# Fused attention and two feed-forward layers: a split first part for two experts instead of one, and an earlier second half of one chunk's routing

## The chip, the core and the metric

The kernel runs on one core of a Trainium2 chip. A core has five engines with instruction queues of their own: TensorE (PE) for matmuls, VectorE (DVE), ScalarE (ACT), GpSimd (POOL) and SyncE (SP), which here only issues DMAs. The metric is the device time of one execution in microseconds (us); lower is better.

## The reference

Attention whose mask keeps a query and a key together only when they fall into the same hash bucket, then a dense feed-forward layer (512 to 2048 to 512), then eight experts of which each token uses two. The last part is where the change lies:

```python
logits = x @ w_gate
noisy_logits = logits + np.log1p(np.exp(x @ w_noise)) * noise
top2 = np.argpartition(-noisy_logits, 2, axis=1)[:, :2]
...
for e in range(E):                       # E = 8, D = 512, F = 1024
    for k in range(2):
        mask = top2[:, k] == e
        h = np.maximum(x[mask] @ w1[e], 0.0)
        out[mask] += top2_w[mask, k, None] * (h @ w2[e])
```

There are 1536 tokens. Which tokens an expert gets is known only once the routing of all tokens is done.

## The kernel before, in words

The tokens go through attention and the dense layer in six chunks of 256, numbered 0 to 5. The program is written out as numbered steps: a table `todo` says which pieces stand in which step (`at`, `soon`, `start`), and from step 100 on each engine runs its instructions in exactly the order in which the steps write them. Nothing overtakes: a wait holds whatever stands behind it on that engine.

**Dense layer.** Sixteen steps per chunk: eight of the first product (`h`, line L455), then eight of the second (`px`, L466, 12 matmuls each). After four `px` steps one half chunk of 128 tokens is ready, and ACT (L480) and DVE (L489) write it to `xr`. SP transposes it to `xrt` (`r_t`, L560), which the routing reads.

**Routing** (`route(ci)`). PE multiplies `xrt` by the gate weights (`pz`, L568 and L570), ACT copies that to `zc` (L573), and a chain of some forty small DVE and ACT instructions (`z` L576, exponentials L585 and L595, `top`, `ix`, the mask `mk` L623, the running count `cum` L625) finds the two experts of each token. PE then counts the earlier tokens of each expert (`pp`, L640 and L641), ACT copies it (`pq`, L643), DVE works out the slots (L645 to `si`, L669), and POOL scatters the rows of `xr` into a table `slots` in DRAM by four indirect DMAs (L675). The second half, from `pp` on, stands in a later step than the first.

**Experts.** Each has 400 slots. `e_load` lets SP fetch an expert's rows transposed as `xg` (L746) and their weights and token numbers as `mt` (L751, L756). `e_meta` (L766 to L776) turns `mt` into scales and indices on DVE. The items of work are listed in `seq`, one after another: for each expert eight `l1` items (`ph`, L789, 12 matmuls each), whose outputs ACT and DVE write to `ht` (L799, L800), and then one `l2` item per 128 slots (`py`, L811, L815), whose output ACT scales (L825) and POOL adds to the result (L828). Three `ph` buffers hold the outputs of `l1` items until DVE has read them.

Expert 0 is cut in two: slots 0 to 255, which `reserve` (L685 to L693) guarantees to be filled by chunks 0 to 4 alone, and slots 256 to 399. So its first part needs no routing of chunk 5. `EA` is the number of experts cut this way. The routing of chunk 5 runs between the first `l1` items, eight small pieces per item from item 2 on.

**Expert weights.** For each expert SP loads eight blocks of 512 KB into four `w32` buffers (`w12_load`, L718 and L721), and `w12_split` turns each into two half-precision parts: ACT the high one (L732), DVE the low one (L733), both named `ew`. `S1` gives the items at which the blocks of expert 1 are split; they are loaded five items earlier.

Of the kernel before, what the change touches and what calls it, by code (L numbers as in the profile page):

```python
# [17 lines left out]
B, H, S, D = 2, 8, 768, 64  # L18
# [15 lines left out]
NCH = NT // CT  # L34
# [17 lines left out]
SW2 = 2.0 ** 6  # L52


PARAM = dict(GM=16, HE=lambda nm, b: 'D', OE=lambda nm, b: 'D', SC=lambda nm, b: 'D', WB=0, XO=lambda b: 'D', NG=16, WS=lambda i: 'P', TS=lambda g: True, XL=lambda g: 'D', GW=2, E0=7, T0=12, T1=16, EL=8, WX=3, PV={(1,2,3):4}, PVD=5, ST={}, VA={}, RA={}, O0=48, OS=2, IS=2, FU=16, VF=2, EC=lambda g: 'AA', QX=8, QS=3, EA=1, S1=(8,8,8,9,9,9,11,13), QE=8, XG=2, XB=2, PC=2, OH=3, BK=3, R0=18, R1=0, LK=8, WL=1, NW=3, LE=lambda nc: nc.scalar, I0=24, LQ=8, LV=0, W=[(g, 1) for g in range(-6, 30)], KA={(0,0,0):-8,(0,0,1):-6,(0,1,0):-4,(0,1,1):-2}, QA={(0,0,0):-7,(0,0,1):-3}, HI=lambda g: 'P', LO=lambda g: False)
PARAM.update(KA={(0, 0, 0): -15, (0, 0, 1): -6, (0, 1, 0): -5, (0, 1, 1): -4, (0, 2, 0): -1, (0, 2, 1): 1, (0, 3, 0): 4, (0, 3, 1): 5, (1, 0, 0): 37, (1, 0, 1): 39, (1, 1, 0): 44, (1, 1, 1): 46, (1, 2, 0): 42, (1, 2, 1): 51, (1, 3, 0): 47, (1, 3, 1): 51}, QA={(0, 0, 0): -15, (0, 0, 1): -3, (0, 0, 2): 1, (0, 0, 3): 3, (0, 1, 0): 8, (0, 1, 1): 9, (0, 1, 2): 17, (0, 1, 3): 21, (0, 2, 0): 24, (0, 2, 1): 28, (0, 2, 2): 30, (0, 2, 3): 33, (1, 0, 0): 37, (1, 0, 1): 41, (1, 0, 2): 47, (1, 0, 3): 52, (1, 1, 0): 57, (1, 1, 1): 56, (1, 1, 2): 60, (1, 1, 3): 69, (1, 2, 0): 72, (1, 2, 1): 69, (1, 2, 2): 80, (1, 2, 3): 84}, VA={(0, 0, 0): -1, (0, 0, 1): -3, (0, 1, 0): -1, (0, 1, 1): -1, (0, 2, 0): 0, (0, 2, 1): 0, (0, 3, 0): -1, (0, 3, 1): -2, (1, 0, 0): -1, (1, 0, 1): -1, (1, 1, 0): 2, (1, 1, 1): -4, (1, 2, 0): -3, (1, 2, 1): -3, (1, 3, 0): 2, (1, 3, 1): -2}, PV={(0, 0, 0): 4, (0, 0, 1): 5, (0, 0, 2): 6, (0, 0, 3): 5, (0, 1, 0): 6, (0, 1, 1): 4, (0, 1, 2): 4, (0, 1, 3): 5, (0, 2, 0): 5, (0, 2, 1): 5, (0, 2, 2): 5, (0, 2, 3): 6, (1, 0, 0): 4, (1, 0, 1): 5, (1, 0, 2): 4, (1, 0, 3): 5, (1, 1, 0): 5, (1, 1, 1): 5, (1, 1, 2): 5, (1, 1, 3): 6, (1, 2, 0): 6, (1, 2, 1): 4, (1, 2, 2): 4, (1, 2, 3): 4}, RA={0: 18, 1: 18, 2: 19, 3: 24, 4: 18}, W=[(g,1) for g in [-6, -4, -3, -1, 0, 0, 1, 1, 2, 4, 4, 7, 8, 8, 9, 10, 11, 12, 13, 14, 15, 16, 16, 17, 18, 20, 20, 22, 22, 23, 23, 24]], EC=lambda g:'AA', LE=lambda nc:nc.sync, HI=lambda g:'AAAA'[g%4], LO=lambda g:[0, 0, 0, 1, 0, 0, 0, 1][g%8]==1, S1=[8, 8, 8, 8, 8, 11, 13, 22], ST={0: 4, 1: 4, 2: 5, 3: 4, 4: 5, 5: 3}, NG=28, WS=lambda i:'PAAA'[i%4], HE=lambda nm,b:'DPDD'[2*(nm=='k')+b], OE=lambda nm,b:'DTDD'[2*(nm=='k')+b], SC=lambda nm,b:'DADD'[2*(nm=='k')+b], R1=2, I0=16, IS=2, O0=56, OS=1, GM=100, BK=3, OH=3, QX=8, QS=2, QE=7, VF=0, T0=12, T1=17, EL=10, WX=5, WL=2, PC=2, GW=2, E0=8, WB=2)


@with_exitstack
def fused(ctx: ExitStack, tc: tile.TileContext, q, k, v, proj, w_in, w_out, w_gate, w_noise, noise,  # L60
          w1, w2, out, dbg=None):
    nc = tc.nc
# [64 lines left out]
    def stack_hi(nm, b, u):
# [17 lines left out]
        if m == "A":
# [64 lines left out]
    FU = PARAM["FU"]  # L210
# [44 lines left out]
    NG = max(PARAM["NG"], FU)  # L255
# [285 lines left out]
    EA = PARAM['EA']  # L541
# [324 lines left out]
    LK, LQ, LV = PARAM["LK"], PARAM["LQ"], PARAM["LV"]  # L866
# [43 lines left out]
    ST = [PARAM["ST"].get(ci, 3 if ci in (0, B * NCH - 1) else PARAM["PVD"] - 1) for ci in range(B * NCH)]  # L910
# [39 lines left out]
    for g in range(g_lo, G1 + 1):  # L950
# [7 lines left out]
        prev = steps.get(g - 1, [])  # L958
# [28 lines left out]
    seq, begin = [], {}  # L987
# [47 lines left out]
    with tc.If(most > CAP):  # L1035
        with tc.tile_pool(name="ov", bufs=1) as ov:
# [10 lines left out]
            x = ov.tile([128, 1024], F32)  # L1047
# [94 lines left out]
```

## Time and profile before

| | us |
|---|---|
| median of 3 runs (829.01 to 832.91) | 829.92 |
| the profiled execution | 827.38 |
| its span, first to last instruction | 825.6 |
| PE busy in the span | 716.3 (87%) |
| DVE busy | 540.1 (65%) |
| ACT busy | 442.2 (54%) |
| POOL busy | 274.8 (33%) |

The profiled execution took 1.8 us more than its span, and lies 2.5 us below the median. Times in rows count from the start of the span. The expert part begins after the last `px` matmul, at about 525 us.

### The profile page before, as it was taken

The numbers are of one execution on the slowest core, as the hardware profiler recorded it, in microseconds if no ns is written. First come the engines' busy times: TensorE is split into PE (matmuls) and PEld (weight loads), VectorE is DVE, ScalarE is ACT, GpSimd is POOL, SyncE is SP. The second block draws the span as 40 slices with busy tenths as digits, with TensorE's granted clock in tenths as the row PEclk, the third lists the DMA queues.
The fourth block names the chain that finished last, engine by engine and source line by source line (L and its number), as shares of the span: only waits on it lengthen the run. The fifth ranks groups of instructions, "written<-read, shape, count | busy, mean of one in ns | idle before, by whom it ended". The sixth has DMA issues, their size and how long they took to land. (4 is left out here: it accounts for less than half of the span.)

```text
span 825.6 us, 14780 instructions
## 1 busy us (share of the span) xinstructions
PE 716.3 (87%) x5398; PEld 445.2 (54%) x5399; DVE 540.1 (65%) x1327; ACT 442.2 (54%) x859; POOL 274.8 (33%) x304
## 2 busy tenths in 40 slices
PE   1466578787988989899999999779999999999995
PEld 1343346544764567476568576447554655555553
DVE  8998479999898889678858625454634526344210
ACT  3677666766776687567557425243533534434220
POOL 6455426653444144314402232241031120311212
PEclk9978689999999999999999999999999999999998
DMA  8999997877988996776685442857966858667213
GB/s 205 238 216 337 325 284 183 204 171 145 185 157 176 214 181 121 179 134 111 132 159 120 96 166 79 229 133 188 254 140 187 187 119 233 142 187 175 28 18 47
DMA packets 268125, 140.03 MB, mean 170 GB/s; under 512 B 224720, under 2 KB 243856, under 8 KB 268048
## 3 DMA queue, kind: packets, MB, share of 16 engines
q1 hardware_dynamic: 261520, 125.37, 63.4%
q0 software_dynamic: 6528, 13.68, 9.3%
q8 instruction: 43, 0.70, 0.4%
q14 instruction: 34, 0.28, 0.1%
HBM read 61.48 MB, written 23.79 MB: 103 GB/s over the span
## 5 line engine op out<-in xcount | busy, mean ns | idle before, releaser
L455 PE MATMUL h<-xt,wi 128*128 128x256 f16 x1152 | 142.3, 279 | 6.7 <-DVE th L485 5.0
L789 PE MATMUL ph<-xg,ew 128*128 128x400 f16 (+2 forms) x864 | 135.4, 320 | 9.3 <-DMA xg<-slots 8.8
L466 PE MATMUL px<-wo,gt 128*128 128x512 f16 x576 | 133.7, 385 | 7.2 <-ACT wo L440 4.2
L733 DVE SCALAR_TENSOR_TENSOR ew<-w,ew 128x1024 f16<-128x1024 f32 x64 | 77.9, 1226 | 89.4 <-ACT ew L732 89.2
L455 PEld LDWEIGHTS <-wi 128*128 128x128 f16 x1152 | 113.0, 100 | 29.2 <-issue 6.5
L811 PE MATMUL py<-ew,ht 128*128 128x512 f16 x576 | 125.8, 379 | 0.0
L828 POOL DMA_INDIRECT out_dram<-yo,ti x32 | 51.2, 1600 | 216.5 <-ACT yo L825 216.5
L251 PE MATMUL s<-kt,qt 128*128 128x512 f16 (+1 forms) x384 | 84.9, 343 | 35.2 <-ACT e L270 26.3
L789 PEld LDWEIGHTS <-ew 128*128 128x128 f16 x864 | 82.8, 100 | 60.2 <-issue 6.7
L270 ACT ACTIVATE e<-s,mx 128x768 f32<-128x768 f32 x96 | 86.0, 897 | 45.8 <-DVE mx L261 38.6
L500 POOL TENSOR_TENSOR gt<-th,gt 128x512 f16<-128x512 f32 x48 | 62.2, 1296 | 113.9 <-ACT gt L499 112.7
L466 PEld LDWEIGHTS <-gt 128*128 128x128 f16 x576 | 55.4, 99 | 72.5 <-issue 10.1
L811 PEld LDWEIGHTS <-ht 128*128 128x128 f16 x576 | 56.3, 98 | 67.0
L260 DVE TENSOR_REDUCE mx<-s 128x1 f32<-128x768 f32 x96 | 90.5, 948 | 2.3 <-PE s L251 2.2
L318 DVE SCALAR_TENSOR_TENSOR er<-e,mx,er 128x768 f16<-128x768 f32 x68 | 72.4, 1069 | 15.2 <-ACT er L309 15.0
L825 ACT ACTIVATE yo<-py,wv 128x512 f32<-128x512 f32 (+1 forms) x32 | 20.3, 634 | 101.9 <-PE py L811 54.5
L309 ACT ACTIVATE er<-e,mx 128x768 f16<-128x768 f32 x68 | 62.9, 933 | 20.1 <-DMA et<-er 9.5
L799 ACT ACTIVATE ht<-ph 128x400 f16<-128x400 f32 (+2 forms) x72 | 33.6, 467 | 73.7 <-PE ph L789 73.7
L251 PEld LDWEIGHTS <-qt 128*128 128x128 f16 x384 | 36.2, 101 | 64.0 <-issue 43.0
L800 DVE SCALAR_TENSOR_TENSOR ht<-ph,ht 128x400 f16<-128x400 f32 (+2 forms) x72 | 37.6, 525 | 49.8 <-ACT ht L799 49.8
L732 ACT ACTIVATE ew<-w 128x1024 f16<-128x1024 f32 x64 | 66.4, 1048 | 2.6 <-DMA w<-in_moe_w_dram 2.6
L363 PE MATMUL pv<-et,vt 128*64 128x256 f16 x720 | 50.6, 281 | 3.2 <-DMA et<-er 3.2
(193 smaller groups left out, 961.5 us busy)
## 6 DMA issues: line engine op xcount, KB each, us to landing
w<-in_moe_w_dram SPq DMA_DIRECT2D x64, 512.0 KB, 4.8
wraw<-in_moe_w_in_dram SPq DMA_DIRECT2D x16, 512.0 KB, 5.1
wraw<-in_moe_w_out_dram SPq DMA_DIRECT2D x16, 512.0 KB, 4.1
slots<-blank SPq DMA_DIRECT2D x6, 1032.0 KB, 11.8
v<-in_v_dram SPq DMA_DIRECT2D x24, 192.0 KB, 3.2
out_dram<-zeros SPq DMA_DIRECT2D x13, 256.0 KB, 6.0
k<-in_k_dram SPq DMA_DIRECT2D x16, 192.0 KB, 3.3
q<-in_q_dram SPq DMA_DIRECT2D x24, 128.0 KB, 2.9
```

The costliest lines, as they stand in the source:

```text
L251: nc.tensor.matmul(ps[:, n0 * 128:n1 * 128], qt[:, s, h, t, :], kt[:, s, h, n0:n1, :].rearrange("p c t -> p (c t)"), start=(s == 0), stop= ...
L260: nc.vector.reduce_max(mx[:, 0:1], st[g]["ps"][:, :S], axis=AX.X)
L270: nc.scalar.activation(e32, st[g]["ps"][:, :S], AF.Exp, scale=0.125, bias=st[g]["mx"][:, 1:2], accum_out=sms[b, cc, hp][:, 2 * h + t:2 * h ...
L309: nc.scalar.activation(er[:, 0], st[g]["e"], AF.Copy, scale=r)
L318: nc.vector.scalar_tensor_tensor(er[:, 1], d["e"], d["mx"][:, 3:4], er[:, 0], op0=OP.mult, op1=OP.subtract)
L455: nc.tensor.matmul(ph[:, a, :], wi[ws][:, d, f0:f0 + 128], xt[:, d, xs, :], start=(d == 0 and ws == 0 and xs == 0), stop=(d == HP - 1 and ...
L466: nc.tensor.matmul(px, gts[ci, f // 2][:, gs, f % 2, t * 128:t * 128 + 128], wo[ws][:, f, :], start=(f == 0 and gs == 0 and ws == 0), stop ...
L500: nc.gpsimd.tensor_tensor(gt[:, 1], th, gt[:, 0], op=OP.subtract)
L732: nc.scalar.activation(hi, x, AF.Copy, scale=SW1 if j == 0 else SW2)
L733: nc.vector.scalar_tensor_tensor(lo, x, SW1 if j == 0 else SW2, hi, op0=OP.mult, op1=OP.subtract)
L789: nc.tensor.matmul(ph[:, :c1 - c0], w[:, ws, d * FE + f * 128:d * FE + f * 128 + 128], xg[e, p][:, xs * HP + d, :], start=(d == 0 and ws = ...
L811: nc.tensor.matmul(py, ht[:, f, hs, t * 128:t * 128 + 128], w[:, ws, f * DM:(f + 1) * DM], start=(i == 0), stop=(i == n - 1))
```

## The change

`EA` goes from 1 to 2: experts 0 and 1 both have a first part of 256 slots. The list of parts was 0 first, 0 rest, 1, 2, ..., 7. It becomes 0 first, 1 first, 0 rest, 1 rest, 2, ..., 7. Chunk 4's routing loses its two free steps: `r1` is 0 for it, so the second half and all that follows (`reserve`, `e_load`, `e_meta`) stand two steps earlier. The splits of expert 1's blocks move from items 8, 8, 8, 8, 8, 11, 13, 22 to items 1, 2, 4, 6, 9, 10, 12, 14, and the splits of expert 2 get places of their own.

```diff
-PARAM = dict(... EA=1, ...)
+PARAM = dict(... EA=2, ...)
-PARAM.update(... S1=[8, 8, 8, 8, 8, 11, 13, 22], ...)
+PARAM.update(... S1=[1, 2, 4, 6, 9, 10, 12, 14], ...)
...
-            r0, r1 = g0 + PARAM["RA"].get(ci, PARAM["R0"]), PARAM["R1"]
+            r0, r1 = g0 + PARAM["RA"].get(ci, PARAM["R0"]), PARAM["R1"] if ci < B * NCH - 2 else 0
...
-        if e >= EA + 1:
-            b0, b1 = begin[prev], begin[e, 0]
-        else:
-            pass
+        if e >= EA:
+            b0, b1 = begin[prev if e > EA else (0, 1)], begin[e, 0]
         for i in range(8):
-            x = b0 + (b1 - b0) * i // 8 if e >= EA + 1 else PARAM["S1"][i]
+            if e < EA:
+                x = PARAM["S1"][i]
+            elif e > EA:
+                x = b0 + (b1 - b0) * i // 8
+            else:
+                x = b0 + 9 + 2 * i if i < 4 else begin[1, 1] + 2 * (i - 1)
             at(x - PARAM['WX'], w12_load, e, i)
             at(x, w12_split, e, i)
     for e, p in gs[EA:]:
         if p == 1:
-            b0 = PARAM["QE"] + e
-            at(b0, done, gen)
+            b0 = PARAM["QE"] if e == 0 else begin[e, 0] + 8
+            if e == 0:
+                at(b0, done, gen)
             at(b0, e_load, e, p)
-            at(b0 + 1, e_meta, e, p)
+            at(begin[e, p] - 3, e_meta, e, p)
```

On PE the 24 `px` matmuls that stood ahead of chunk 4's `pp` now stand behind it, ahead of the same chunk's `reserve`.

On SP, from the last weight blocks of expert 0 to the first of expert 1, the program before has these rows (the second `xrt` is the last half of chunk 5):

```order
L721 DMA w_6799<-in_moe_w_dram 128x2x512
L560 DMA_TRANSPOSE xrt<-xr 128x8x128
L746 DMA_TRANSPOSE xg<-slots 128x8x256
L751 DMA mt<-slots 128x2x8
L560 DMA_TRANSPOSE xrt<-xr 128x8x128
L718 DMA w_7006<-in_moe_w_dram 128x1024
```

The changed program has these in the same place:

```order
L721 DMA w_6829<-in_moe_w_dram 128x2x512
L746 DMA_TRANSPOSE xg<-slots 128x8x256
L751 DMA mt<-slots 128x2x8
L746 DMA_TRANSPOSE xg<-slots 128x8x256
L751 DMA mt<-slots 128x2x8
L560 DMA_TRANSPOSE xrt<-xr 128x8x128 x2
L718 DMA w_6926<-in_moe_w_dram 128x1024
```

Both halves of chunk 5's `xrt` now stand behind the fetches of both first parts, and expert 1's loads behind them.

On DVE, around the end of the dense layer, the difference reads so (`w_6806` and `w_6829` are the last two blocks of expert 0, `w_6926` is the first of expert 1, L489 is the last half of chunk 5, and `z` is the start of its routing):

```order
+L772 TENSOR_TENSOR wv<-wv 128x2
+L733 SCALAR_TENSOR_TENSOR ew<-w_6806,ew 128x1024
+L733 SCALAR_TENSOR_TENSOR ew<-w_6829,ew 128x1024
+L489 SCALAR_TENSOR_TENSOR xr<-px,xr 128x512
 L800 SCALAR_TENSOR_TENSOR ht<-ph,ht 128x256
+L733 SCALAR_TENSOR_TENSOR ew<-w_6926,ew 128x1024
 L576 TENSOR_TENSOR z<-zc 128x32
 L582 SCALAR_TENSOR_TENSOR rw<-z 128x16
```

The first row ends the second `e_meta`. Before, the two splits and L489 stood ahead of the only `e_meta`; now they stand behind two of them, and an expert 1 split stands ahead of `z`.

On ACT, in the same place (`zc` starts the routing of chunk 5, L595 are its exponentials):

```order
 L799 ACTIVATE ht<-ph 128x256
+L732 ACTIVATE ew<-w_6926 128x1024
 L573 ACTIVATE zc<-pz 128x64
 L585 ACTIVATE rw<-rw 128x16
 L799 ACTIVATE ht<-ph 128x256
+L732 ACTIVATE ew<-w_6928 128x1024
```

Four splits of expert 1 now stand within the routing of chunk 5, where before there was none.

## Rows read from the trace of the kernel before

**Rows 1.** PE's timeline: start, us, instruction, count, [idle before, and its releaser].

```profile
512.09 0.17 PE L640 MATMUL pp<-mk,before 128*128 128x16 f16 x1
...
517.34 7.93 PE L466 MATMUL px<-wo,gt 128*128 128x512 f16 x36
529.45 4.46 PE L789 MATMUL ph<-xg,ew 128*128 128x256 f16 x24 [4.18 <-DMA xg<-slots]
533.75 0.26 PE L568 MATMUL pz<-wg,xrt 128*128 128x32 f16 x4
...
539.96 2.78 PE L789 MATMUL ph<-xg,ew 128*128 128x256 f16 x24
542.58 10.52 PE L811 MATMUL py<-ew,ht 128*128 128x512 f16 x48
557.68 6.18 PE L789 MATMUL ph<-xg,ew 128*128 128x144 f16 x72 [4.58 <-DMA xg<-slots]
564.42 3.69 PE L789 MATMUL ph<-xg,ew 128*128 128x144 f16 x36 [0.55 <-DVE ht L800]
...
576.00 16.40 PE L789 MATMUL ph<-xg,ew 128*128 128x400 f16 x96
```

**Rows 2.** DVE's timeline, from chunk 4's mask to its slots.

```profile
507.54 1.33 DVE L733 SCALAR_TENSOR_TENSOR ew<-w,ew 128x1024 f16<-128x1024 f32 x1 [1.65 <-ACT ew L732]
...
509.49 0.16 DVE L625 TENSOR_TENSOR cum<-cum,mk 128x8 f16<-128x8 f16 x1
...
514.66 0.16 DVE L645 TENSOR_SCALAR d<-d 128x2 f32<-128x2 f32 x1
...
516.22 0.17 DVE L669 CAST si<-sf 128x4 int32<-128x4 f32 x1
```

**Rows 3.** The chain in order of time: start, us, what (scatter landing, then fetch landing).

```profile
521.09 4.28 DMA slots<-xr,si
525.38 4.02 DMA xg<-slots
```

**Rows 4.** SP's queue in its timeline (SPq), after the scatter has landed.

```profile
525.38 1.99 SPq L746 DMA_TRANSPOSE xg<-slots  x1
527.41 0.58 SPq L751 DMA_DIRECT2D mt<-slots  x1
528.09 1.24 SPq L560 DMA_TRANSPOSE xrt<-xr  x1
529.38 2.01 SPq L718 DMA_DIRECT2D w<-in_moe_w_dram  x4
```

**Rows 5.** DVE's timeline, from the last half chunk to the end of chunk 5's routing.

```profile
525.94 0.69 DVE L489 SCALAR_TENSOR_TENSOR xr<-px,xr 128x512 f16<-128x512 f32 x1 [3.72 <-ACT xr L480]
529.86 0.17 DVE L766 TENSOR_SCALAR wv<-mt 128x2 f32<-128x2 f32 x1 [3.23 <-DMA mt<-slots]
...
530.33 0.16 DVE L772 TENSOR_TENSOR wv<-wv 128x2 f32<-128x2 f32 x1
...
534.59 0.19 DVE L576 TENSOR_TENSOR z<-zc 128x32 f32<-128x32 f32 x1 [2.17 <-ACT zc L573]
...
542.14 0.17 DVE L669 CAST si<-sf 128x4 int32<-128x4 f32 x1
```

**Rows 6.** Landing lines of the views of `xrt` and of L718.

```profile
DMA to landing us min/median/max: 3.0/3.0/3.1
DMA to landing us min/median/max: 3.5/4.5/5.4
```

**Rows 7.** Groups by line and shape: count, busy us, mean ns, idle before.

```profile
L733 DVE SCALAR_TENSOR_TENSOR ew<-w,ew 128x1024 f16<-128x1024 f32 x64 | 77.9, 1226 | 89.4 <-ACT ew L732 89.2
L732 ACT ACTIVATE ew<-w 128x1024 f16<-128x1024 f32 x64 | 66.4, 1048 | 2.6 <-DMA w<-in_moe_w_dram 2.6
```

**Rows 8.** Windows, L789 alone: PE and weight loads busy (count), clock granted, DMA share, GB/s.

```profile
561.00:562.00 1.00, 1.00 (x19) 1.00 (x17) 1.00 1.28 290
```

**Rows 9.** Windows, all engines (PE, PEld, DVE, ACT, POOL; clock, DMA share, GB/s).

```profile
530.00:535.00 5.00, 5.00 (x45) 3.89 (x43) 1.29 (x9) 0.61 (x2) 0.00 (x0) 0.66 0.93 327
```

More of the change, by code (lines that the diff above doesn't have):

```diff
@@ L52 @@
 SW2 = 2.0 ** 6
-PARAM = dict(GM=16, HE=lambda nm, b: 'D', OE=lambda nm, b: 'D', SC=lambda nm, b: 'D', WB=0, XO=lambda b: 'D', NG=16, WS=lambda i: 'P', TS=lambda g: True, XL=lambda g: 'D', GW=2, E0=7, T0=12, T1=16, EL=8, WX=3, PV={(1,2,3):4}, PVD=5, ST={}, VA={}, RA={}, O0=48, OS=2, IS=2, FU=16, VF=2, EC=lambda g: 'AA', QX=8, QS=3, EA=1, S1=(8,8,8,9,9,9,11,13), QE=8, XG=2, XB=2, PC=2, OH=3, BK=3, R0=18, R1=0, LK=8, WL=1, NW=3, LE=lambda nc: nc.scalar, I0=24, LQ=8, LV=0, W=[(g, 1) for g in range(-6, 30)], KA={(0,0,0):-8,(0,0,1):-6,(0,1,0):-4,(0,1,1):-2}, QA={(0,0,0):-7,(0,0,1):-3}, HI=lambda g: 'P', LO=lambda g: False)
@@ L56 @@
-PARAM.update(KA={(0, 0, 0): -15, (0, 0, 1): -6, (0, 1, 0): -5, (0, 1, 1): -4, (0, 2, 0): -1, (0, 2, 1): 1, (0, 3, 0): 4, (0, 3, 1): 5, (1, 0, 0): 37, (1, 0, 1): 39, (1, 1, 0): 44, (1, 1, 1): 46, (1, 2, 0): 42, (1, 2, 1): 51, (1, 3, 0): 47, (1, 3, 1): 51}, QA={(0, 0, 0): -15, (0, 0, 1): -3, (0, 0, 2): 1, (0, 0, 3): 3, (0, 1, 0): 8, (0, 1, 1): 9, (0, 1, 2): 17, (0, 1, 3): 21, (0, 2, 0): 24, (0, 2, 1): 28, (0, 2, 2): 30, (0, 2, 3): 33, (1, 0, 0): 37, (1, 0, 1): 41, (1, 0, 2): 47, (1, 0, 3): 52, (1, 1, 0): 57, (1, 1, 1): 56, (1, 1, 2): 60, (1, 1, 3): 69, (1, 2, 0): 72, (1, 2, 1): 69, (1, 2, 2): 80, (1, 2, 3): 84}, VA={(0, 0, 0): -1, (0, 0, 1): -3, (0, 1, 0): -1, (0, 1, 1): -1, (0, 2, 0): 0, (0, 2, 1): 0, (0, 3, 0): -1, (0, 3, 1): -2, (1, 0, 0): -1, (1, 0, 1): -1, (1, 1, 0): 2, (1, 1, 1): -4, (1, 2, 0): -3, (1, 2, 1): -3, (1, 3, 0): 2, (1, 3, 1): -2}, PV={(0, 0, 0): 4, (0, 0, 1): 5, (0, 0, 2): 6, (0, 0, 3): 5, (0, 1, 0): 6, (0, 1, 1): 4, (0, 1, 2): 4, (0, 1, 3): 5, (0, 2, 0): 5, (0, 2, 1): 5, (0, 2, 2): 5, (0, 2, 3): 6, (1, 0, 0): 4, (1, 0, 1): 5, (1, 0, 2): 4, (1, 0, 3): 5, (1, 1, 0): 5, (1, 1, 1): 5, (1, 1, 2): 5, (1, 1, 3): 6, (1, 2, 0): 6, (1, 2, 1): 4, (1, 2, 2): 4, (1, 2, 3): 4}, RA={0: 18, 1: 18, 2: 19, 3: 24, 4: 18}, W=[(g,1) for g in [-6, -4, -3, -1, 0, 0, 1, 1, 2, 4, 4, 7, 8, 8, 9, 10, 11, 12, 13, 14, 15, 16, 16, 17, 18, 20, 20, 22, 22, 23, 23, 24]], EC=lambda g:'AA', LE=lambda nc:nc.sync, HI=lambda g:'AAAA'[g%4], LO=lambda g:[0, 0, 0, 1, 0, 0, 0, 1][g%8]==1, S1=[8, 8, 8, 8, 8, 11, 13, 22], ST={0: 4, 1: 4, 2: 5, 3: 4, 4: 5, 5: 3}, NG=28, WS=lambda i:'PAAA'[i%4], HE=lambda nm,b:'DPDD'[2*(nm=='k')+b], OE=lambda nm,b:'DTDD'[2*(nm=='k')+b], SC=lambda nm,b:'DADD'[2*(nm=='k')+b], R1=2, I0=16, IS=2, O0=56, OS=1, GM=100, BK=3, OH=3, QX=8, QS=2, QE=7, VF=0, T0=12, T1=17, EL=10, WX=5, WL=2, PC=2, GW=2, E0=8, WB=2)
@@ new lines @@
+PARAM = dict(GM=16, HE=lambda nm, b: 'D', OE=lambda nm, b: 'D', SC=lambda nm, b: 'D', WB=0, XO=lambda b: 'D', NG=16, WS=lambda i: 'P', TS=lambda g: True, XL=lambda g: 'D', GW=2, E0=7, T0=12, T1=16, EL=8, WX=3, PV={(1,2,3):4}, PVD=5, ST={}, VA={}, RA={}, O0=48, OS=2, IS=2, FU=16, VF=2, EC=lambda g: 'AA', QX=8, QS=3, EA=2, S1=(8,8,8,9,9,9,11,13), QE=8, XG=2, XB=2, PC=2, OH=3, BK=3, R0=18, R1=0, LK=8, WL=1, NW=3, LE=lambda nc: nc.scalar, I0=24, LQ=8, LV=0, W=[(g, 1) for g in range(-6, 30)], KA={(0,0,0):-8,(0,0,1):-6,(0,1,0):-4,(0,1,1):-2}, QA={(0,0,0):-7,(0,0,1):-3}, HI=lambda g: 'P', LO=lambda g: False)
@@ new lines @@
+PARAM.update(KA={(0, 0, 0): -15, (0, 0, 1): -6, (0, 1, 0): -5, (0, 1, 1): -4, (0, 2, 0): -1, (0, 2, 1): 1, (0, 3, 0): 4, (0, 3, 1): 5, (1, 0, 0): 37, (1, 0, 1): 39, (1, 1, 0): 44, (1, 1, 1): 46, (1, 2, 0): 42, (1, 2, 1): 51, (1, 3, 0): 47, (1, 3, 1): 51}, QA={(0, 0, 0): -15, (0, 0, 1): -3, (0, 0, 2): 1, (0, 0, 3): 3, (0, 1, 0): 8, (0, 1, 1): 9, (0, 1, 2): 17, (0, 1, 3): 21, (0, 2, 0): 24, (0, 2, 1): 28, (0, 2, 2): 30, (0, 2, 3): 33, (1, 0, 0): 37, (1, 0, 1): 41, (1, 0, 2): 47, (1, 0, 3): 52, (1, 1, 0): 57, (1, 1, 1): 56, (1, 1, 2): 60, (1, 1, 3): 69, (1, 2, 0): 72, (1, 2, 1): 69, (1, 2, 2): 80, (1, 2, 3): 84}, VA={(0, 0, 0): -1, (0, 0, 1): -3, (0, 1, 0): -1, (0, 1, 1): -1, (0, 2, 0): 0, (0, 2, 1): 0, (0, 3, 0): -1, (0, 3, 1): -2, (1, 0, 0): -1, (1, 0, 1): -1, (1, 1, 0): 2, (1, 1, 1): -4, (1, 2, 0): -3, (1, 2, 1): -3, (1, 3, 0): 2, (1, 3, 1): -2}, PV={(0, 0, 0): 4, (0, 0, 1): 5, (0, 0, 2): 6, (0, 0, 3): 5, (0, 1, 0): 6, (0, 1, 1): 4, (0, 1, 2): 4, (0, 1, 3): 5, (0, 2, 0): 5, (0, 2, 1): 5, (0, 2, 2): 5, (0, 2, 3): 6, (1, 0, 0): 4, (1, 0, 1): 5, (1, 0, 2): 4, (1, 0, 3): 5, (1, 1, 0): 5, (1, 1, 1): 5, (1, 1, 2): 5, (1, 1, 3): 6, (1, 2, 0): 6, (1, 2, 1): 4, (1, 2, 2): 4, (1, 2, 3): 4}, RA={0: 18, 1: 18, 2: 19, 3: 24, 4: 18}, W=[(g,1) for g in [-6, -4, -3, -1, 0, 0, 1, 1, 2, 4, 4, 7, 8, 8, 9, 10, 11, 12, 13, 14, 15, 16, 16, 17, 18, 20, 20, 22, 22, 23, 23, 24]], EC=lambda g:'AA', LE=lambda nc:nc.sync, HI=lambda g:'AAAA'[g%4], LO=lambda g:[0, 0, 0, 1, 0, 0, 0, 1][g%8]==1, S1=[1, 2, 4, 6, 9, 10, 12, 14], ST={0: 4, 1: 4, 2: 5, 3: 4, 4: 5, 5: 3}, NG=28, WS=lambda i:'PAAA'[i%4], HE=lambda nm,b:'DPDD'[2*(nm=='k')+b], OE=lambda nm,b:'DTDD'[2*(nm=='k')+b], SC=lambda nm,b:'DADD'[2*(nm=='k')+b], R1=2, I0=16, IS=2, O0=56, OS=1, GM=100, BK=3, OH=3, QX=8, QS=2, QE=7, VF=0, T0=12, T1=17, EL=10, WX=5, WL=2, PC=2, GW=2, E0=8, WB=2)
```

## The prediction

> **What bounds the kernel now.** I read three views in this order. The table by engine says PE is busy for 87% of the span, so first look for where PE is not. PE's timeline around the start of the expert part has the answer: two large holes, 4.18 us before the first `l1` item and 4.58 us before the rest of expert 0, both ended by the landing of an `xg` fetch, and one of 0.55 us behind DVE [rows 1]. The chain in order of time then shows what is late: the scatter of chunk 4 lands 4.28 us after its last issue, and the fetch takes another 4.02 us [rows 3]. The timelines of DVE and SP, last, tell what else stands in those queues [rows 2, 4, 5]. After a hole the clock suffers as well: in the five microseconds after the first one the mean granted clock was 0.66, that is, mostly the lower of the two levels [rows 9], and 24 matmuls took 4.46 us, against 2.78 at the full clock [rows 1].
>
> So the holes and their low clock cost 4.18 + 1.7, 4.58 + 1.9 and 0.55 us, 12.9 together, and nothing else in this stage is to be won. For the 1.9: 72 matmuls of 144 columns took 6.18 us [rows 1], and at the full clock the rate is some 17 weight loads in 1 us [rows 8], or about 60 ns each, 4.3 us for 72.
>
> **The cut of expert 1.** It replaces 96 matmuls of 400 columns (16.40 / 96 = 171 ns) by 96 of 256 (2.62 / 24 = 109 ns, from 539.96 to 542.58) and 96 of 144 (60 ns) [rows 1, 8]. 109 + 60 is 169, so the cut costs PE nothing. Its `l2` items are the same in number.
>
> **Chunk 4's routing, two steps earlier.** A `px` step is 2.6 us (7.93 for three), so `pp`, at 512.09, could start at 506.9 [rows 1]. But the running count that it reads is written by DVE at 509.49 and done at 509.65, behind a weight split that itself waited for ACT [rows 2], and nothing ahead of these moves. So PE waits there for 2.7 us where it was busy, and the last `px` ends at 528.0, not 525.3. The chain gains only 2.4 us. Behind `pp`, ACT makes one split (1.05) and DVE one (1.23) [rows 7], so L645 starts at about 512.3; from there to the slots takes 1.7 (514.66 to 516.39) [rows 2]: `si` ends at 514.0, 2.4 earlier. The scatter then lands at 523.0 and the fetch at 527.0 [rows 3], a microsecond before PE asks for it. The first hole is gone.
>
> **What is late next.** SP must now issue two fetches and two `mt` before chunk 5's `xrt`. From 523.0: `xg` 1.99, `mt` 0.58, `xg` 1.99, with gaps, so the second `mt` is issued at 527.7 [rows 4]. The first one was used 2.45 us after its issue (527.41 to 529.86) [rows 4, 5], so the second `e_meta` starts at 530.2 and takes 0.6 (529.86 to 530.49). On DVE stand behind it two splits of expert 0 (2 x 1.23) and then L489 (0.69), the last half of chunk 5 [rows 5, 7]: done at 533.9. Only then can SP issue the last `xrt`, which lands 3.0 us later [rows 6], at 536.9. PE, having started at 528.0 and made 24 matmuls at 109 ns, stands at `pz` from 530.6 on. It waits 6.3 us, and with it everything behind `pz`. `pz` comes at 536.9 where it came at 533.75. Bounds: if `mt` is there 1 us sooner or later, so is `pz`.
>
> That nothing on DVE passes a waiting instruction is plain from the row: at 529.86 it had idled 3.23 us for `mt` [rows 5]. The Trainium skill's page TensorE: Matmul & The Clock Gate (section Part 1, on engine queues) says so as a rule: ACT and DVE are strictly first in, first out, only PE takes weight loads out of turn. If instead L489 could pass the second `e_meta`, `xrt` would go out right behind the second `mt`, land at 531.3, and the sum below would be some 5.6 us lower; I take the row.
>
> **The splits inside chunk 5's routing.** SP is free for expert 1's loads only after that last `xrt`, at 535.2. They land 3.5 to 5.4 us after issue, median 4.5 [rows 6], the first at 539.7. Its ACT half (1.05) stands ahead of `zc`, its DVE half (1.23) ahead of `z` [rows 7]: `z` at 542.0, 5.1 us after `pz`, where it came 0.84 us after it. From `z` to the end of `si` took 7.7 us (534.59 to 542.31) [rows 5]; three more DVE splits add 3.7, and an ACT split ahead of the exponentials 1.05: 12.4, so `si` ends at 554.4. Meanwhile PE can't run ahead. There are three `ph` buffers, and the `ht` instructions that free them stand between the pieces of the routing. The eighth `l1` item needs the buffer of the fifth. Before, it ended 0.27 us after `si` (542.58 against 542.31) [rows 1, 5]; now one more split (1.23) stands between the `ht` that frees that buffer and `si`, so it ends about 1 us ahead of `si`, at 553.4. **Here the change is 10.8 us behind.** Bounds: 7.5 if the loads take 3.5 us and the ACT halves hide, 13.5 if they take 5.4 and each split waits for its load.
>
> **What it gets back.** Chunk 5's slots are known at 554.4. From `si` to the last scatter's landing took chunk 4 9.0 us (516.39 to 525.37), and the fetch 4.0 [rows 2, 3], so `xg` for the rest of expert 0 is there at 567.4. PE needs it after two `l2` items of 5.26 (10.52 for two [rows 1]), expert 1's eight `l1` items (10.5) and two more `l2` items, at about 585. So the second hole goes, with over 15 us to spare: 4.58 + 0.55 + 1.9 = 7.0 back. Against that stand new small waits, some 3.3 us in all, where one split (1.05 and 1.23) now stands ahead of an `ht` that PE waits for: at the first item of expert 1 (0.4), at the `l2` of both first parts (0.5 and 0.8), and in the rest of expert 1 (1.6), whose `l1` items are only 0.72 us long and share DVE with expert 2's splits; I got these by laying the queues side by side with the durations above. Bounds 0 to 6. And one fall of the clock, after the last wait of the slow stretch: 1.7; bounds 0 to 3.4. The falls within the stretch cost nothing, since DVE sets the pace there.
>
> **The sum.** +10.8 - 7.0 + 3.3 + 1.7 = +8.8 us. On the profiled execution (825.6 of span, 827.38 in all) that is 836.2; the median of the runs is 2.5 us higher, so I predict 839. From `l1` of expert 2 on, both kernels do the same.
>
> **Rivals.** *Both holes go and nothing replaces them.* That needs the last `xrt` to land by 530.6, 6.3 us sooner than I work out, so `mt` of expert 1 landing by 524. Then only the 2.7 us at `pp` and a clock fall are lost: 829.9 - 12.9 + 2.7 + 1.7 = 821. For it: the scatter is the releaser of both holes [rows 3], and the new order gives the second one 15 us of cover. Against it: the order of SP and DVE. The Trainium skill's page DMA: Bandwidth & Descriptors (Rules for kernel authors) advises just this, issue the DMA early, compute, wait late; by that rule alone this rival, 821, is the outcome. The trace does not bear it out for this kernel: SP issued the last `xrt` only behind the fetch and the `mt` (528.09), though DVE had finished its input at 526.63 [rows 4, 5]. *The wait at `pz` comes, but the splits are hidden.* Then the 10.8 shrinks to about 4, since DVE idled 2.17 us ahead of `z` and 3.72 ahead of L489 before [rows 5]; +2.5, 832.5. Against it: loads that start at 535.2 can't land by 537. *The loads are slower.* With 5.4 us and four of them competing with the fetches, each split waits, and the clock falls again: +15, 845. *The earlier second half brings nothing:* it is in my sum, since `pp` gains 2.4 of 5.2 us and PE pays 2.7 for it.
>
> **How the numbers follow.** My forecast 0.67 (834 to 844), slow loads 0.13 (844 to 851), splits hidden 0.12 (830 to 834), no new waits 0.08 (818 to 828). The range 831 to 848 leaves out the last rival, the top of the slow loads and the bottom of the hidden splits, 0.2 together. A measurement of this kernel tells 0.5%, 4.1 us, from no change. Faster by more: 0.08, the last rival. Within: up to 834.1, nearly all of the hidden splits, 0.12. Slower: 0.80.
>
> **What the changed profile would show.** Right: PE waits 2 to 3 us at `pp` of chunk 4 for DVE; no hole before the first `l1` item; 24 matmuls, then a wait of about 6 us at `pz` for `xrt`; DVE idle until the second `mt`, then two splits and L489; `zc` about 4 us behind `pz`; waits of PE for `ht` in the first part; no hole before the rest of expert 0. Wrong: `pz` following its 24 matmuls at once, `si` of chunk 5 before 548, or a hole of over 2 us later than 560, in the rest of expert 1 or ahead of expert 2, where I put only small waits.

## The result and the profile after

Over eight runs each, the changed kernel takes 837.83 us in the median (834.47 to 839.49), the kernel before 829.9 (828.91 to 832.91): ratio 1.0083, 95% interval 1.0062 to 1.0104. It is 8 us slower. Its profiled execution took 834.47 us with a span of 832.7, against 827.38 and 825.6 before, thus 7.1 us more.

All of that lies in one stage, from the first `px` of chunk 5 to the `l1` items behind expert 1's last `l2` (they are expert 2's; its first item was already pulled ahead, in both kernels). Before, PE's timeline has these at 504.32 and 610.61, 106.3 us apart; after, at 504.25 and 617.70, 113.45 apart. From there to the end of the span both take 215.0. The lengths below are counted from that first `px`, since what comes ahead of it differs from one execution to the next, whatever the kernel: in the fourteen profiled ones it came between 502.69 and 507.89.

Three lines of PE's timeline of before, beside those of [rows 1]:

```profile
504.32 7.93 PE L466 MATMUL px<-wo,gt 128*128 128x512 f16 x36
...
512.14 5.34 PE L466 MATMUL px<-wo,gt 128*128 128x512 f16 x24
...
610.61 16.41 PE L789 MATMUL ph<-xg,ew 128*128 128x400 f16 x96
```

PE's timeline of after (start, us, instruction, count, idle before and its releaser), to be laid beside [rows 1]:

```profile
504.25 2.75 PE L466 MATMUL px<-wo,gt 128*128 128x512 f16 x12
509.44 0.18 PE L640 MATMUL pp<-mk,before 128*128 128x16 f16 x1 [2.44 <-DVE mk L623]
...
509.66 7.03 PE L466 MATMUL px<-wo,gt 128*128 128x512 f16 x24
...
516.56 13.11 PE L466 MATMUL px<-wo,gt 128*128 128x512 f16 x60
535.94 5.20 PE L789 MATMUL ph<-xg,ew 128*128 128x256 f16 x24 [6.27 <-DVE xr L489]
540.97 0.26 PE L568 MATMUL pz<-wg,xrt 128*128 128x32 f16 x4
...
545.15 1.47 PE L789 MATMUL ph<-xg,ew 128*128 128x256 f16 x12 [0.99 <-DVE ht L800]
548.09 1.47 PE L789 MATMUL ph<-xg,ew 128*128 128x256 f16 x12 [1.47 <-DVE ht L800]
551.45 0.18 PE L640 MATMUL pp<-mk,before 128*128 128x16 f16 x1 [1.89 <-DVE mk L623]
...
555.59 10.52 PE L811 MATMUL py<-ew,ht 128*128 128x512 f16 x48
565.95 8.02 PE L789 MATMUL ph<-xg,ew 128*128 128x256 f16 x72
574.42 1.47 PE L789 MATMUL ph<-xg,ew 128*128 128x256 f16 x12 [0.45 <-DVE ht L800]
...
586.09 0.91 PE L789 MATMUL ph<-xg,ew 128*128 128x144 f16 x12
...
603.94 3.22 PE L789 MATMUL ph<-xg,ew 128*128 128x144 f16 x48 [0.63 <-DVE ht L800]
607.65 2.19 PE L789 MATMUL ph<-xg,ew 128*128 128x400 f16 x12 [0.49 <-ACT ht L799]
...
617.70 16.41 PE L789 MATMUL ph<-xg,ew 128*128 128x400 f16 x96
```

Both waits for `xg` are gone: the rest of expert 0 starts at 586.09 with no idle time ahead of it. In their place stands one wait of 6.27 us ahead of the first `l1` item, ended by DVE's L489, and then three of 1 to 1.9 us in the first part of expert 0. Its first `l2` comes at 555.59, where it came at 542.58 [rows 1].

DVE's timeline of after, beside [rows 2, 5], shows what L489 stood behind:

```profile
513.79 0.17 DVE L669 CAST si<-sf 128x4 int32<-128x4 f32 x1
...
530.01 0.17 DVE L766 TENSOR_SCALAR wv<-mt 128x2 f32<-128x2 f32 x1 [6.74 <-DMA mt<-slots]
...
532.38 0.17 DVE L766 TENSOR_SCALAR wv<-mt 128x2 f32<-128x2 f32 x1 [1.73 <-DMA mt<-slots]
...
532.92 2.36 DVE L733 SCALAR_TENSOR_TENSOR ew<-w,ew 128x1024 f16<-128x1024 f32 x2
535.20 0.68 DVE L489 SCALAR_TENSOR_TENSOR xr<-px,xr 128x512 f16<-128x512 f32 x1
...
542.48 1.22 DVE L733 SCALAR_TENSOR_TENSOR ew<-w,ew 128x1024 f16<-128x1024 f32 x1 [2.95 <-ACT ew L732]
543.63 0.18 DVE L576 TENSOR_TENSOR z<-zc 128x32 f32<-128x32 f32 x1
...
555.23 0.17 DVE L669 CAST si<-sf 128x4 int32<-128x4 f32 x1
```

DVE idles 6.74 us for the first `mt` and 1.73 for the second. Where the 6.74 comes from, the chain in order of time tells (start, us, what), beside [rows 3]:

```profile
518.78 5.78 DMA slots<-xr,si
524.58 2.10 SPq L746
526.73 0.57 SPq L751
527.34 2.59 SPq L746
529.98 2.37 DMA mt<-slots
```

The slots were known 2.4 us earlier, but the last scatter took 5.78 us to land, not 4.28, so the fetch starts at 524.58 instead of 525.38.

Windows (PE, PEld, DVE, ACT, POOL; then granted clock, DMA share, GB/s) around the two longest waits:

```profile
508.00:515.00 7.00, 5.54 (x19) 2.19 (x20) 5.41 (x22) 2.16 (x4) 0.76 (x1) 0.76 0.48 133
536.00:541.00 5.00, 5.00 (x25) 3.45 (x25) 0.42 (x1) 0.39 (x1) 0.00 (x0) 0.51 0.79 195
```

A clock of 0.51 means that the 24 matmuls behind the long wait ran almost wholly at 1.2 GHz, the lower level: 5.20 us in place of 2.78. Behind `pp`, 24 `px` matmuls took 7.03 us; before, the same 24 took 5.34 (512.14), in a stretch where the granted clock was 1.00, that is 2.4 GHz.

### The profile page after: what moved, and what is told of

It reads as the page before. It is cut to its first block, busy times and chain, and to the rows that moved or that the text cites. A ratio compares the mean times of both kernels' runs of the same rounds, so it can differ in the third digit from the quotient of the medians.

```text
span 832.7 us, 14995 instructions
## 1 busy us (share of the span) xinstructions
PE 717.3 (86%) x5494; PEld 452.6 (54%) x5495; DVE 540.2 (65%) x1341; ACT 442.2 (53%) x867; POOL 272.4 (33%) x304
## 5 line engine op out<-in xcount | busy, mean ns | idle before, releaser
L789 PE MATMUL ph<-xg,ew 128*128 128x400 f16 (+2 forms) x960 | 135.7, 303 | 10.3 <-DVE xr L489 6.3
L789 PEld LDWEIGHTS <-ew 128*128 128x128 f16 x960 | 87.7, 99 | 56.8 <-issue 12.8
L251 PE MATMUL s<-kt,qt 128*128 128x512 f16 (+1 forms) x384 | 87.8, 352 | 35.4 <-ACT e L270 25.2
L800 DVE SCALAR_TENSOR_TENSOR ht<-ph,ht 128x400 f16<-128x400 f32 (+2 forms) x80 | 38.5, 487 | 50.9 <-ACT ht L799 50.7
```

Of the source, the lines that this page charges most:

```text
L251: nc.tensor.matmul(ps[:, n0 * 128:n1 * 128], qt[:, s, h, t, :], kt[:, s, h, n0:n1, :].rearrange("p c t -> p (c t)"), start=(s == 0), stop= ...
L789: nc.tensor.matmul(ph[:, :c1 - c0], w[:, ws, d * FE + f * 128:d * FE + f * 128 + 128], xg[e, p][:, xs * HP + d, :], start=(d == 0 and ws = ...
```

## The experiments

Twelve kernels, each timed against the kernel before on the same chip. From row to row only the ratios compare: the kernel before had medians of 828.5 to 829.9 on the different chips. Lengths are from the first `px` of chunk 5 to the first `l1` item, to the first `l2` and to the `l1` items behind expert 1's last `l2`, in one profiled execution each; the clock behind the wait at `pp` alone makes 1.7 us of difference between executions (see the end).

| kernel | median, us | ratio to before (95%) | first `l1` | first `l2` | behind expert 1 |
|---|---|---|---|---|---|
| before | 829.9 | | 25.1 | 38.3 | 106.3 |
| after | 837.83 | 1.0083 (1.0062 to 1.0104) | 31.7 | 51.3 | 113.5 |
| `meta_late` | 831.45 | 1.0023 (1.0000 to 1.0046) | 27.5 | 49.9 | 111.4 |
| `r1_back` | 830.64 | 1.0009 (0.9987 to 1.0031) | 25.1 | 48.0 | 109.5 |
| `splits_out` | 832.37 | 1.0047 (1.0029 to 1.0066) | 30.9 | 44.7 | 109.6 |
| `one_r1_0` | 831.91 | 1.0037 (1.0019 to 1.0054) | 29.3 | 42.0 | 110.6 |
| `both` | 826.2 | 0.9977 (0.9957 to 0.9997) | 26.7 | 39.6 | 104.6 |
| `both_r1_1` | 827.96 | 0.9992 (0.9973 to 1.0011) | 26.2 | 39.6 | 104.9 |
| `both_mask` | 828.14 | 0.9984 (0.9962 to 1.0005) | 23.1 | 40.7 | 105.9 |
| `one_r1_0_late` | 827.84 | 0.9988 (0.9970 to 1.0006) | 27.5 | 39.2 | 107.2 |
| `both_tail` | 825.58 | 0.9964 (0.9944 to 0.9983) | 25.1 | 40.5 | 104.9 |
| `both_tail_r1_1` | 826.52 | 0.9970 (0.9950 to 0.9990) | 25.5 | 38.7 | 102.7 |
| `w32_5` | 823.19 | 0.9918 (0.9895 to 0.9941) | 26.8 | 38.5 | 101.4 |
| `load7_late` | 826.83 | 0.9968 (0.9950 to 0.9986) | 26.8 | 38.6 | 103.8 |

**One part at a time, and one suspected cost at a time.** `meta_late` is after with the two first-part `e_meta` behind chunk 5's routing:

```diff
-                    at(r0 + PARAM["E0"] + 2 + r1, e_meta, e, 0)
...
+    for e in range(EA):
+        at(7 + 2 * e, e_meta, e, 0)
```

> The changed kernel with one thing moved: the two e_meta of the first parts stand on DVE behind chunk 5's routing (items 7 and 9), no longer ahead of the last two splits of expert 0 and of L489. Theory A (DVE held L489, the last half chunk, behind the second e_meta's wait for mt, and the first l1 item waits for L489): the wait of 6.27 us ahead of the first l1 item falls to about 1.3 us (ACT's and DVE's copy of the last half, 0.6 + 0.69), the first l1 item starts near 531 instead of 535.94, and the time falls by 4 to 5 us, to about 833. Theory B (PE waits for the two fetches themselves, which SP issues ahead of the last xrt): the first l1 item still starts after 535, and the time stays at 837 to 838.

PE's timeline of `meta_late`:

```profile
533.33 2.78 PE L789 MATMUL ph<-xg,ew 128*128 128x256 f16 x24 [1.41 <-DVE xr L489]
...
543.61 2.72 PE L789 MATMUL ph<-xg,ew 128*128 128x256 f16 x12 [3.35 <-DVE ht L800]
```

The wait falls from 6.27 to 1.41 us, so `e_meta` was what held L489. The first `l2` hardly moves (49.9 for 51.3), because now the splits in chunk 5's routing are late by themselves: PE waits 3.35 us for an `ht` behind one. The two delays lie partly side by side.

`r1_back` is after with chunk 4's two free steps back, `PARAM["R1"]` for every chunk.

> The changed kernel with chunk 4's two free steps given back (two experts still cut). Theory A (the earlier second half makes PE wait 2.44 us at pp for the mask and lowers its clock after that, and it puts both e_meta ahead of L489): no wait at pp, the last px ends at 525.3 instead of 529.7, L489 stands ahead of the e_meta again, and the hole before the first l1 item is that of the kernel before (4 to 5 us, ended by xg). The splits inside the routing stay, so the first part of expert 0 still ends some 8 us later than in the kernel before: about 834 to 835. Theory B (the earlier second half is a gain of 2.4 us in the chain of the scatter, and the rest is the cost): slower than the changed kernel by 2 us, 840.

PE's timeline of `r1_back`:

```profile
529.35 4.46 PE L789 MATMUL ph<-xg,ew 128*128 128x256 f16 x24 [4.10 <-DMA xg<-slots]
...
540.26 2.72 PE L789 MATMUL ph<-xg,ew 128*128 128x256 f16 x12 [2.88 <-DVE ht L800]
```

Two cut experts alone give the first hole as before, a first `l2` 9.8 us later, and 6.5 of that back by the second hole. The time is 830.64, better than the first theory expected and far from the second's 840.

`splits_out` is after with expert 1's splits behind the routing and its first `l1` item not pulled ahead of expert 0's `l2`:

```diff
-        if n and (p == 0 or n > EA):
+        if n > 1 and (p == 0 or n > EA):
...
-S1=[1, 2, 4, 6, 9, 10, 12, 14]
+S1=[8, 8, 8, 8, 9, 10, 12, 14]
```

> The changed kernel with the first four splits of expert 1 at item 8, behind chunk 5's routing, and its first l1 item not pulled ahead of expert 0's l2 items, so that they hide behind these (10.5 us of PE). Theory A (each split in the routing delays it, and with it the ht that free PE's buffers): the wait before the first l1 item stays at 6 us, but the stretch from pz to the end of expert 0's eighth l1 item falls from 14.6 us to about 8.8, and the time to about 831.5. Theory B (the splits fill time in which DVE was waiting anyway): nothing gained, and 0.9 us lost ahead of expert 0's first l2 item, 838 to 839.

PE's timeline of `splits_out`:

```profile
533.81 5.20 PE L789 MATMUL ph<-xg,ew 128*128 128x256 f16 x24 [5.61 <-DVE xr L489]
...
569.27 1.47 PE L789 MATMUL ph<-xg,ew 128*128 128x256 f16 x12 [1.92 <-DVE ht L800]
```

From the first `pz` to the first `l2` it takes 8.8 us, as before, instead of 14.6: the splits cost 5.8 there. Behind expert 1 only 3.8 are left. Expert 1 now waits 1.92 us for an `ht` behind the split of its last `w2` block, whose load stands on SP behind the fetch for the rest of expert 0: issued at 562.44, 14.8 us behind the first `l2`, where after had 12.2.

`one_r1_0` is the kernel before with the earlier second half alone, the line with `r1` of the diff.

> The kernel before with one part of the change alone: chunk 4's second half two steps earlier, one expert cut, splits where they were. Theory A (PE pays 2.44 us and a fall of the clock at pp, and the only e_meta now stands ahead of the last splits and L489): the hole before the first l1 item stays at about 4 us, now ended by L489 at about 533.5, and the time is 2 to 4 us above the kernel before, 832 to 834. Theory B (the scatter lands 2.4 us earlier and the first hole shrinks by that): 827 to 828.

PE's timeline of `one_r1_0`:

```profile
535.26 4.11 PE L789 MATMUL ph<-xg,ew 128*128 128x256 f16 x24 [4.83 <-DVE xr L489]
...
563.16 10.97 PE L789 MATMUL ph<-xg,ew 128*128 128x144 f16 x108 [4.62 <-DMA xg<-slots]
```

The earlier half chunk makes the kernel 0.37% slower by itself: the hole behind `xg` turns into one behind L489, and the second hole stays. The two halves of the change cost 4.3 and 3.2 us of the stage, together near the 7.2 of after; by the ratios 0.46% of 0.83%, with intervals that just meet, so whether a microsecond or two comes only from both together stays open.

**The repairs together.** `both` is `meta_late` and `splits_out` in one.

> The changed kernel with both repairs together: the two first-part e_meta behind chunk 5's routing, and expert 1's weight splits and first l1 item out of that routing. Times are on a kernel before of 829.9 us. Theory A (two separate costs, the wait for L489 ahead of the first l1 item and the splits inside chunk 5's routing, which add up): the wait ahead of the first l1 item is under 1.5 us, pz to the first l2 item is 9 us or less as in the kernel before, no hole over 2 us ahead of the rest of expert 0, and 827 to 829 us, about 2 us under the kernel before. Theory B (the queues of DVE hand the lateness on: what leaves chunk 5's routing is missing ahead of expert 1's own items): a wait of 4 us or more for ht or ew in the first part of expert 1, and 831 us or more.

PE's timeline of `both`:

```profile
529.59 2.78 PE L789 MATMUL ph<-xg,ew 128*128 128x256 f16 x24 [1.41 <-DVE xr L489]
...
564.28 1.47 PE L789 MATMUL ph<-xg,ew 128*128 128x256 f16 x12 [2.09 <-DVE ht L800]
```

The gains more than add on the profiled executions: 8.8 us of the stage against after, where `meta_late` alone had 2.0 and `splits_out` 3.8. By the ratios they add within the noise (1.06% against 0.60% and 0.36%). The time is 826.2, a little under the 827 to 829 expected and just below the kernel before. Of the wait of 4 us or more that the second theory had in expert 1, 2.09 us came.

`both_r1_1` is `both` with `r1` 1 for chunk 4.

> As both, with one of the two free steps back between chunk 4's pieces. Theory A (the half chunk moved earlier gains what the mask and the running count on DVE allow, 2.4 us, so one step of 2.6 us does as well as two and PE doesn't stand at pp): the wait at pp is under 0.5 us, the fetch still lands before PE needs it or at most 1 us later, and the time is 1 to 2 us under both. Theory B (two steps are worth twice one): the hole of 2 us or more ahead of the first l1 item is back, ended by xg, and the time is 1 to 2 us over both.

PE's timeline of `both_r1_1`:

```profile
509.51 0.17 PE L640 MATMUL pp<-mk,before 128*128 128x16 f16 x1 [0.56 <-DVE mk L623]
...
529.77 4.08 PE L789 MATMUL ph<-xg,ew 128*128 128x256 f16 x24 [4.32 <-DMA xg<-slots]
```

The wait at `pp` goes, but the hole behind `xg` is back. The time fell on the second theory's side (827.96), though the intervals overlap.

`both_mask` is `both` with expert 0's splits and its later loads one step later:

```diff
-        at(NU + 11 + i, w12_split, 0, i)
+        at(NU + 12 + i, w12_split, 0, i)
...
-            at(NU + 11 + i, w12_load, 0, i + 4)
+            at(NU + 12 + i, w12_load, 0, i + 4)
```

> As both, with expert 0's weight splits and the four later loads one step later, so that on DVE chunk 4's mask and running count stand ahead of a split. Theory A (the wait of 2.4 us at pp is the split ahead of the mask): pp follows its px at once or with a wait under 0.5 us, the clock doesn't fall there, and the time is 2 to 4 us under both. Theory B (the split isn't what the mask waits for, or its delay is paid at the end of expert 0's splits): the wait at pp stays over 2 us, or a wait of 2 us or more for a weight split stands ahead of the first l1 or l2 item; same as both or slower.

PE's timeline of `both_mask`:

```profile
528.72 4.45 PE L789 MATMUL ph<-xg,ew 128*128 128x256 f16 x24 [2.17 <-DMA xg<-slots]
536.70 0.29 PE L568 MATMUL pz<-wg,xrt 128*128 128x32 f16 x4 [3.16 <-DMA xrt<-xr]
```

`pp` waits no longer, so the split ahead of the mask was its cause. PE reaches the first `l1` sooner (23.1, the earliest of all), but no time is gained: it waits there for the fetch, and the later load now stands between the two `xrt` on SP, so that `pz` waits 3.16 us. Neither theory had that.

`one_r1_0_late` is `one_r1_0` with `e_meta` late.

> The kernel before (one expert with a first part) with chunk 4's second half two steps earlier and e_meta of expert 0 behind chunk 5's routing. On a kernel before of 829.9 us. Theory A (the wait of 4.83 us that the earlier half chunk alone brought ahead of the first l1 item is e_meta waiting for mt ahead of L489, also with one expert): that wait is under 1.5 us, the hole of 4.6 us ahead of the rest of expert 0 stays, and 827 to 829 us. Theory B (the wait is chunk 5's own routing, which has less time): it stays at 3 us or more and the time is 831 to 832 us.

PE's timeline of `one_r1_0_late`:

```profile
535.34 2.78 PE L789 MATMUL ph<-xg,ew 128*128 128x256 f16 x24 [1.41 <-DVE xr L489]
...
562.38 6.06 PE L789 MATMUL ph<-xg,ew 128*128 128x144 f16 x72 [4.78 <-DMA xg<-slots]
```

The first theory holds with one expert as well: 4.83 us become 1.41, and the ratio falls from 1.0037 to 0.9988.

**The last hole, and the late landing.** `both_tail` is `both` with `S1=[8, 8, 8, 8, 9, 9, 10, 11]`, `both_tail_r1_1` the same with `r1` 1.

> As both, with expert 1's last three w2 splits one to three items earlier, so that the last w2 load is issued ahead of the fetch for the rest of expert 0 and not behind it. Against a kernel before of 829 us, and both at 826.2. Theory A (the one new hole in both, 2.09 us for ht in the first part of expert 1, is a DVE split that waits for a load queued on SP behind that fetch, which itself waits for chunk 5's scatter): the hole is under 0.5 us, and 824 to 825 us, 2 us under both. Theory B (the hole is DVE's work itself, the splits among the ht): it stays at 1.5 us or more, one or two items sooner, and the time is that of both.

> As both_tail, with one of the two free steps back in chunk 4's routing. Theory A (what r1 = 1 saves at pp, 2 to 3 us, it pays at the first l1 item, where it waited 4.3 us for xg in the run of both_r1_1 against 1.4 for L489 in both): within 0.2% of both_tail. Theory B (the wait for xg was a slow fetch of that one execution): the wait is under 2.5 us and the time 1.5 us or more under both_tail.

PE's timeline of `both_tail`:

```profile
532.52 0.27 PE L568 MATMUL pz<-wg,xrt 128*128 128x32 f16 x4 [1.75 <-DMA xrt<-xr]
...
560.50 5.40 PE L789 MATMUL ph<-xg,ew 128*128 128x256 f16 x48 [1.39 <-DVE ht L800]
```

That settled little: the hole shrank to 1.39 us, between the two theories, because the load, issued by 549.9, was still waited for at 557.8. The time is that of `both` within the intervals. `both_tail_r1_1` had 4.36 us behind `xg` and no wait at `pp`, and the time of `both_tail`, as its first theory said.

`w32_5` is `both_tail` with one more buffer for weight blocks, `load7_late` is `both_tail` with one load out of the way:

```diff
-        x = m2.tile([128, 1024], F32, name="w32", bufs=4)
+        x = m2.tile([128, 1024], F32, name="w32", bufs=5)
```

```diff
-    for i in range(8):
+    for i in range(7):
         at(NU + 11 + i, w12_split, 0, i)
-        if i < 4:
+        if i < 3:
             at(NU + 11 + i, w12_load, 0, i + 4)
...
+    at(0, w12_load, 0, 7)
+    at(7, w12_split, 0, 7)
```

> As both_tail, with five buffers for weight blocks in place of four; nothing else moves. In every run with chunk 4's second half earlier, its slots were known 1.7 to 2.4 us sooner than in the kernel before, yet SP issued the fetch at 19.7 to 21.4 us behind the start of chunk 4's px, against 21.1 before, because the last scatter landed 5 to 6 us after its issue instead of 4.3. Theory A (expert 0's last weight load, which waits for a buffer until after the scatters have begun, takes the DMA engines from them): with a fifth buffer that load is issued before the scatters, the last one lands 4.3 to 4.8 us after its issue, the fetch is issued at 19.3 us or sooner, and 1 to 2 us are gained over both_tail (824 us where the kernel before has 828.5). Theory B (the landing is set by the four scatters themselves or by other traffic): the landing stays over 5.5 us and the time is that of both_tail.

> As both_tail, with expert 0's last w2 load behind the first-part fetches on SP and its split behind chunk 5's routing, so that neither stands ahead of chunk 5's last half. Theory A (the load collides with chunk 4's scatters): the last scatter lands 4.3 to 4.8 us after its issue, the fetch is issued at 19.3 us or sooner, and up to 2 us are gained over both_tail, unless the split then makes PE wait ahead of the first l2 item. Theory B (the scatters land late whatever is loaded): landing over 5.5 us, and the time is that of both_tail or up to 2 us more, by the later split.

The landing lines of the view of `slots`: first `w32_5`, from the issue of the last scatter (520.30) to the fetch (524.09), then `load7_late`, where the last scatter, issued at 519.36, let the fetch go at 522.93:

```profile
DMA to landing us min/median/max: 3.8/3.8/3.8
```

```profile
DMA to landing us min/median/max: 3.6/4.4/5.3
```

With that load away from the last scatter, in two different ways (in `w32_5` its issue moves from 1.3 us ahead of that scatter to 3.7, in `load7_late` to behind the fetch), the last scatter lands 3.8 and 3.6 us after its issue instead of 5.9 in `both_tail`, and the fetch is issued 18.3 and 18.1 us behind the first `px` instead of 20.5. So expert 0's last weight load was what slowed it.

In `both_mask` and `both_r1_1` the landing took 5.9 and 6.4 us though that load was out of the way. What moved beside the scatter there, the DMA view shows for the stretch from the last scatter's issue to its landing: packets, MB and share of the 16 engines' time in the queue of SP's transfers, first `both_tail` (517.40 to 523.30), then `both_mask` (518.54 to 524.43), then `both_r1_1` (519.22 to 525.62):

```profile
q1 hardware_dynamic: 290, 0.54, 27.5%
q1 hardware_dynamic: 255, 0.49, 29.0%
q1 hardware_dynamic: 1057, 0.26, 58.0%
```

In `both_mask` most of another weight block of expert 0, issued at 516.16, took its place. In `both_r1_1` it is 0.26 MB in 1057 packets, the size of a transposed half chunk (`xrt`, issued at 516.81); `both_tail_r1_1` has the same and 6.5 us. All fourteen kernels fall in line: 3.6 to 4.3 us with at most 0.02 MB beside the scatter (`before`, `r1_back`, `w32_5`, `load7_late`), 5.2 to 6.2 with about one weight block, 6.4 and 6.5 with the `xrt`. For the `xrt` no run takes it away alone.

At the first `l1` item the earlier fetch gains nothing: in both runs it still waits 1.41 us for L489, the copy of the last half chunk, and starts at 26.8. But the `xrt` behind the fetches goes out 24.4 and 24.5 us behind the first `px` instead of 26.4, and `pz`, which waited 1.75 and 0.86 us for it in `both_tail`, waits no longer: the first `l2` comes at 38.5 and 38.6 instead of 40.5. `w32_5` gains 1.5 us more behind that, because expert 1's `w2` loads find a buffer sooner and the holes in expert 1 vanish; `load7_late` has two of 1.0 and 1.1 us there. `w32_5`, at 0.9918, beats both kernels. No run has the fifth buffer in the kernel before, or both repairs with the two free steps back, so how much of that gain belongs to the second cut and how much to the earlier half stays open.

## Why the prediction was right, and where it was off

The forecast of 839 us, slower, came out by the mechanism it named: the second `mt` holds `e_meta`, this holds L489, and the splits of expert 1 then lengthen chunk 5's routing. `meta_late`, `splits_out` and `both` take each away in turn. By its own steps:

- **The cut of expert 1, nothing.** Right: 12 matmuls of 256 columns stay at 1.3 us, and those of 144 columns ran 96 in 6.16 us, 64 ns each: 109 + 64 against 171.
- **The wait at `pp`, 2.7 us; `si` at 514.0.** 2.44, and 513.96. Missing was the clock: it fell behind that wait, `px` ended at 529.67, not 528.0.
- **The scatter lands at 523.0.** This term failed: 524.58. I took the 9.0 us from `si` to landing over from [rows 2, 3], but expert 0's last weight load, whose buffer comes free 4.4 us later (519.16, before 514.77), now runs beside the scatters. Of the 2.4 us gained at the slots 0.8 reached the fetch.
- **The second `mt` at 527.7, L489 done at 533.9.** 529.98 and 535.88, by the late scatter (1.6) and a second fetch of 2.59 us on SP in place of 1.99.
- **A wait of 6.3 us at `pz`.** One of 6.27 came, but that the sizes agree is chance: it is another wait. It stands ahead of the first `l1` item, where I had no hole, and L489 released it, not the `xrt`. The first `ph` takes the PSUM space that `px` leaves, by the order in which the program closes and opens the pools (read from the kernel); after and eight of the experiments show L489 as the releaser. Before, `xg` was later still and hid it. So the 24 matmuls that I let run ahead of the wait ran behind it, at the lower clock, and `pz` came at 540.97, not 536.9, with no wait of its own.
- **First `l2` +10.8 us.** +13.0, within the bounds of 7.5 to 13.5: loads issued at 537.20 for 535.2, `z` at 543.63 for 542.0, `si` done at 555.4 for 554.4, and `l2` just behind it rather than 1 us ahead. In parts it was less close: `pz` came 7.2 us later than before where I had 3.1, and from `pz` to the first `l2` the splits cost 5.8 where I had 7.7, since the first block landed 0.4 us behind `pz`, not 2.8 (`z` 2.7 us behind `pz`, not 5.1).
- **Gets back 7.0, pays 3.3 and 1.7.** The second hole went; the fetch was issued at 563.84, 22 us ahead of its use. Only 1.57 us of small waits came, and no fall of the clock later: from the first `l2` to the `l1` items behind expert 1 it took 62.1 us instead of 68.0, 5.9 back where I had a net 2.0. They were 0.45 in the first part of expert 1 and 0.63 and 0.49 toward the end of its rest; at its first item and at the `l2` of both first parts, where I had 1.7, the `ht` was early enough.

So +13.0 - 5.9 = +7.1 on the profiled execution, for +8.8: two parts were off by 2.2 and 3.9 us in opposite directions, so that the total came so close is in part luck. In the rival with hidden splits the sum is +2.0 (4 - 7.0 + 3.3 + 1.7), not +2.5; nothing hangs on that. The rival with no new waits (821) needed the new waits away, and with them away `w32_5`, which has a fifth buffer besides, is at 0.9918 of before, 823.

## What to carry to other kernels

When a piece of work is moved earlier, follow it to the instruction that consumes it: here 2.4 us at the slots became 0.8 at the fetch, because a weight load ran beside the last scatter. An instruction that waits for a DMA (`e_meta`) belongs behind whatever else on its queue is ready, above all behind the last input of the next stage; that alone was worth 0.6% here. Two delays that lie side by side hide each other: taking one away showed less than its share at the place where they end (2.0 and 3.8 us, 8.8 together). Both repairs brought the change just under the kernel before (0.9977), and with one more buffer it was a clear gain (0.9918).

## What the runs showed of the hardware beside that

The clock after a wait of PE is not set by the length of the wait alone. At the same place, the 24 `px` behind `pp` took 7.03 us in `meta_late` after a wait of 3.15 us and 5.34 in `one_r1_0` after one of 3.15; 6.86 in `both` and 5.34 in `both_tail` after 2.4. Behind 1.41 us the first 24 `l1` matmuls took 2.78 us in all six runs that had it, behind 4.1 to 6.3 us between 4.08 and 5.20; but 2.17 us in `both_mask` gave 4.45. What decides between them the rows don't show.
